# Attention steps reordered: the scores first, three kinds of transposes and small products behind them, the weighted sums last

## The chip, the cores and the metric

The kernel runs on one core of one Trainium2 chip. The metric is the time of one execution on the device, in microseconds (us). The engines are named as the profile names them: PE is TensorE's matrix multiplication, PEld its weight loads, DVE is VectorE, ACT is ScalarE, POOL is GpSimd, SP is SyncE, which here only issues DMAs.

## The reference

Three layers follow one another. Windowed attention has 4 batches, 8 heads, 576 positions and heads of 64; a position sees itself and the 63 before it. Its output, 2304 tokens of 512 columns, goes through a mixture of 8 experts, in which a token whose skip score is not positive keeps its value, and then through a block of two products.

```python
def _attn_ref(q, k, v):
    scores = scale * np.matmul(q, k.transpose(0, 1, 3, 2))
    mask = (rel >= 0) & (rel < window)
    scores = np.where(mask, scores, -1000000000.0)
    scores = scores - np.max(scores, axis=-1, keepdims=True)
    attn = np.exp(scores)
    attn = attn / (np.sum(attn, axis=-1, keepdims=True) + 1e-09)
    return np.matmul(attn, v).astype(np.float32)

def _moe_ref(x, w_skip, w_gate, w1, w2):
    do_compute = x @ w_skip > 0
    xc = x[do_compute]
    logits = xc @ w_gate
    e_idx = np.argmax(logits, axis=1)
    gate_w = probs[np.arange(len(xc)), e_idx]
    h = np.maximum(xc[mask] @ w1[e], 0.0)
    y[mask] = gate_w[mask, None] * (h @ w2[e])
    out[do_compute] = xc + y

def _moe2_ref(x, w_in, w_out):
    h = x @ w_in
    g = np.where(pos, h, np.where(neg, 0.0, (h + beta) ** 2 / (4.0 * beta)))
    return g @ w_out
```

## The kernel before

**Stages.** The attention takes the first 104 us, the experts the time to 340 us, the block the rest. All three stand in one program whose order on each engine is the order in which the code is written. The attention works in 18 steps `t` (NT = 18), one for each 128 tokens; a step's two groups of 64 tokens have the numbers 2t and 2t + 1 (`k` is 0 or 1). Work on one tile of tokens is spread over several steps, a few functions to each:

- `stage_s(t)`, the scores: masks by four bf16 products (L343), 32 products of 64 rows by 64 columns of q against the keys (L353), into two of three PSUM banks `s0` to `s2`; then on VectorE the row maxima (L360), one instruction for each group, and on ScalarE eight exponentials (L364) that take the maximum as bias.
- `stage_t(t)`: eight fp32 transposes of the probabilities (L378) into banks `pt0` and `pt1`. The copy of the first bank into SBUF (`pts`, group 2t, "even") is ScalarE's (L382), that of the second ("odd") VectorE's (L384). For tile 15 ScalarE makes both.
- `stage_v(t)`: 32 products of the transposed probabilities with the values `vt` (L406), 128 rows by 64 columns, into bank `o`; a column of ones in `vt` gives the row sums. VectorE normalises: `den` (L412), its reciprocal, a product into `x`. Then the loads of two further blocks of values go on SP's queue into the buffers just read (L313).
- `stage_x(t)`: four transposes of `x` (L429) into a score bank, copied to `xT` by VectorE (L437).
- `stage_l(t)`: four products of `xT` with the gate weights (L450), the logits, copied by VectorE (`ls`, L458). `stage_l2(t)`: one product that adds up their quarters (L464) into the bank `misc`.
- The ranks, for groups of 3, 3, 3, 4, 2 and 3 tiles (ROUTES): `route_a`, six VectorE operations from the logits to a one-hot choice (from L472), in steps 7, 10 and 13; a step later `route_b`, small products against a triangular matrix (L500 to L503) and four VectorE operations (L527 to L542) and `route_h`, GpSimd's selection tiles, and in the same step the gate, `route_g`, two VectorE operations from L575 on; three steps after `route_a` `route_c`, products (L604) and a sum. So `route_b` is in steps 8, 11 and 14 and `route_c` in 10, 13 and 16.

The fp32 transposes and the gate's products use the array in one tiling (128*128, the logits 128*32), the scores 64*64, the weighted sums 128*64: the profile prints that form in each row.

**The order of a step.** TensorE runs, in step t of the loop: weighted sums of tile t - 3, probability transposes of t - 2, rank products that are due, scores of t, the quarters' sum of t - 5, logits of t - 4, transposes of x of t - 3. VectorE and ScalarE have the matching order. Scaling of q for the next block (L328, ScalarE) stands ahead of the scores in the odd steps. At a step's end the loads of raw weights go on SP's queue, and in steps 3, 5, 6, 8, 9, 11, 12, 14 and 15 a finished load is split (L140 on ScalarE, the rest on GpSimd). The loop runs to step 16; step 17 and what remains of the pipeline are written out behind it.

```python
        for t in range(NT - 1):
            if t >= 3:
                stage_v(t - 3)
            if t >= 2:
                stage_t(t - 2)
            for f in due.pop(t, ()):
                f()
            if t % 2:
                scale_q(t // 2 + 1)
            stage_s(t)
```

Ahead of the loop 114 small products (WARM, L621) run while the first loads are under way.

## Time and profile before

| what | value |
| --- | --- |
| runs without a profile | 693.84, 694.4 and 698.65 us (median 694.4) |
| the profiled execution | 691.08 us, its span 689.3 us |
| PE busy | 661.5 us, 96% of the span |
| DVE busy | 427.6 us, 62% |
| ACT busy | 385.6 us, 56% |
| POOL busy | 93.2 us, 14% |
| mean granted TensorE clock | 0.999 |

The profile lists what each engine did in one execution. A busy share says how much of the span an engine worked, not what it waited for. The span runs from the first instruction to the last; the execution's time is 1.8 us longer. In the timeline a row is one stretch of like instructions: start, length, engine, line, operation, output and inputs by the program's names, form, count, and in brackets how long the engine stood idle ahead of it and what ended that. "issue" there means that nothing the profile shows was waited for. Lengths of matmuls that follow one another overlap, so the pace of TensorE is read from differences of starts.

### The profile page before, as it was taken

What the parts mean: (1) busy time and instruction counts of PE and PEld (TensorE: products, weight loads), DVE (VectorE), ACT (ScalarE), POOL (GpSimd) and SP (SyncE); (2) the same over time, 40 slices, a digit from 0 to 9 for tenths busy, and PEclk for the clock granted to TensorE, in tenths of its full rate; (3) what the DMA queues carried; (4) which work ended last, traced back from release to release, by engine and by line L of the source; (5) the groups of instructions that cost most, each with busy time, mean ns of one, the idle gap of its engine ahead of it and who ended that gap; (6) DMA issues with size and microseconds to landing.
All of it is one profiled execution on the core that took longest, in us unless ns stands there. A gap on an engine that the chain in (4) does not pass through costs nothing.

```text
span 689.3 us, 12283 instructions
## 1 busy us (share of the span) xinstructions
PE 661.5 (96%) x4633; PEld 567.9 (82%) x4633; DVE 427.6 (62%) x814; ACT 385.6 (56%) x769; POOL 93.2 (14%) x140
## 2 busy tenths in 40 slices
PE   7999989999989989989999999999999999999997
PEld 6787867777767766979899999999999999999995
DVE  5788876995963997877888844343434333433332
ACT  6787744763824773666666655454444454445442
POOL 3256546232312110000000000000000000000000
PEclk9999999999999999999999999999999999999999
DMA  8999838997872855323424003030300030002001
GB/s 258 291 276 295 256 116 287 325 341 252 283 294 69 281 216 191 112 87 108 123 92 138 1 1 76 16 78 16 92 1 0 1 93 0 1 1 47 0 1 46
DMA packets 34584, 88.93 MB, mean 129 GB/s; under 512 B 7014, under 2 KB 8166, under 8 KB 34500
## 3 DMA queue, kind: packets, MB, share of 16 engines
q1 hardware_dynamic: 26352, 74.34, 34.8%
q10 hardware_dynamic: 5748, 6.83, 3.1%
q0 software_dynamic: 2400, 6.68, 2.7%
q8 instruction: 48, 0.79, 0.5%
q14 instruction: 36, 0.29, 0.1%
HBM read 75.91 MB, written 13.12 MB: 129 GB/s over the span
## 4 chain that ended last, share of the span: by engine, by line
PE 52%; DVE 6%; ACT 2%; issue 1%; DMA 0%; ACTq 0%; DVEq 0%
PE po L1005 25%; PE h L977 25%; DVE c L998 2%; PE spare L1093 1%; ACT q L988 1%; DVE gs L996 1%; PE p2x L967 1%; DVE c L995 1%; DVE w L141 1%; DVE q L987 1%; DVE q L991 1%; DVE x2T L136 0%; DMA x<-x 0%; ACT q L984 0%; ACT gs L993 0%
## 5 line engine op out<-in xcount | busy, mean ns | idle before, releaser
L977 PE MATMUL h<-x2T,w 128*128 128x384 f32 x1152 | 218.0, 337 | 1.1 <-DVE x2T L136 1.1
L1005 PE MATMUL po<-w,gs 128*128 128x512 f32 x864 | 217.0, 395 | 1.7 <-ACT w L140 0.9
L977 PEld LDWEIGHTS h<-x2T,w 128*128 128x128 f32 x1152 | 204.5, 188 | 10.1 <-DVE x2T L136 1.7
L1005 PEld LDWEIGHTS po<-w,gs 128*128 128x128 f32 x864 | 159.5, 188 | 32.1 <-ACT w L140 1.2
L984 ACT ACTIVATE q<-h 128x384 f32<-128x384 f32 x96 | 46.9, 489 | 107.9 <-PE h L977 104.0
L987 DVE TENSOR_SCALAR q<-q 128x384 f32<-128x384 f32 x96 | 34.4, 358 | 97.9 <-ACT q L984 97.8
L991 DVE TENSOR_TENSOR q<-hs,q 128x384 f32<-128x384 f32 x96 | 53.7, 559 | 49.8 <-ACT q L988 49.8
L993 ACT ACTIVATE gs<-q 128x384 fp32r<-128x384 f32 x96 | 50.4, 525 | 60.0 <-DVE q L991 60.0
L996 DVE TENSOR_TENSOR gs<-q,gs 128x384 fp32r<-128x384 f32 x96 | 53.7, 559 | 44.3 <-ACT gs L993 44.3
L852 PE MATMUL y<-w,hT 128*128 128x512 f32 x264 | 70.2, 403 | 4.0 <-DVE hT L136 2.7
L140 ACT ACTIVATE w<-raw 128x1024 fp32r<-128x1024 f32 x64 | 65.4, 1058 | 15.4 <-PEq L924 4.7
L141 DVE TENSOR_TENSOR w<-raw,w 128x1024 fp32r<-128x1024 f32 x55 | 64.8, 1219 | 3.8 <-ACT w L140 1.9
L988 ACT ACTIVATE q<-q 128x384 f32<-128x384 f32 x96 | 50.5, 526 | 22.3 <-DVE q L987 18.8
L852 PEld LDWEIGHTS y<-w,hT 128*128 128x128 f32 x264 | 47.2, 188 | 17.2 <-DVE hT L136 4.4
L364 ACT ACTIVATE pr<-s,nb 128x128 f32<-128x128 f32 x144 | 39.0, 384 | 15.5 <-DVE nb L360 15.5
L986 ACT ACTIVATE hs<-h 128x384 f32<-128x384 f32 x96 | 46.8, 488 | 0.0
L813 PE MATMUL ha<-w,mxT 128*128 128x512 f32 x132 | 33.4, 399 | 3.5 <-DVE mxT L136 0.7
L813 PE MATMUL hb<-w,mxT 128*128 128x512 f32 x132 | 34.9, 400 | 0.0
L813 PEld LDWEIGHTS ha<-w,mxT 128*128 128x128 f32 x132 | 23.9, 188 | 12.2 <-issue 4.5
L777 POOL DMA_INDIRECT x<-mx,idx x11 | 16.5, 1497 | 105.4 <-POOLq L921 41.0
L360 DVE TENSOR_REDUCE nb<-s 128x4 f32<-128x512 f32 x36 | 23.2, 686 | 11.4 <-PE s L353 10.2
L813 PEld LDWEIGHTS hb<-w,mxT 128*128 128x128 f32 x132 | 24.0, 188 | 4.7
(182 smaller groups left out, 683.3 us busy)
## 6 DMA issues: line engine op xcount, KB each, us to landing
raw<-in_wu SPq DMA_DIRECT2D x62, 512.0 KB, 6.7
raw<-in_wd SPq DMA_DIRECT2D x31, 512.0 KB, 4.1
x<-x SPq DMA_DIRECT2D x21, 256.0 KB, 3.2
vt<-in_vs SPq DMA_DIRECT2D x36, 130.0 KB, 6.2
out<-out SPq DMA_DIRECT2D x36, 128.0 KB, 2.3
q<-in_qs SPq DMA_DIRECT2D x8, 512.0 KB, 5.2
kt<-in_ks SPq DMA_DIRECT2D x8, 512.0 KB, 6.8
x<-x ACTq DMA_DIRECT2D x16, 256.0 KB, 6.4
```

The costliest lines, as they stand in the source:

```text
L140: nc.scalar.activation(t[:, 0], src, AF.Copy)
L141: eng.tensor_tensor(t[:, 1], src, t[:, 0].bitcast(F32), ALU.subtract)
L813: nc.tensor.matmul(ph, lhsT=xT[:, a, c, :], rhs=halves[4 * e + j, c][:, b, :], start=(n == 0), stop=(n == len(seq) - 1),)
L852: nc.tensor.matmul(py, lhsT=hT[j][:, a, c, :], rhs=halves[4 * e + 2 + j, c][:, b, :], start=(j == 0 and n == 0), stop=(j == 1 and n == len ...
L977: nc.tensor.matmul(ph, lhsT=halves[U_IN + m // 4, c][:, b, (m % 4) * P : (m % 4 + 1) * P], rhs=xT[:, a, c, :], start=(n == 0), stop=(n == ...
L984: nc.scalar.activation(q, ph, AF.Relu, bias=0.5, scale=0.5)
L986: nc.scalar.activation(h, ph, AF.Copy)
L988: nc.scalar.activation(q, q, AF.Square)
L991: nc.vector.tensor_tensor(q, h, q, ALU.max)
L993: nc.scalar.activation(gs[:, 0], q, AF.Copy)
L996: dve.tensor_tensor(gs[:, 1], q, gs[:, 0].bitcast(F32), ALU.subtract)
L1005: nc.tensor.matmul(po[i], lhsT=gs[:, a, i * P : (i + 1) * P], rhs=w[:, b, :], start=(m == m0 and (a, b) == PASSES[0]), stop=(m == m1 - 1 a ...
```

## The change

The scores' stage is cut into three functions: `stage_s` keeps the products, `stage_m(t, k)` is one row maximum, `stage_e(t)` the exponentials. `stage_t` takes a function `between`, which it calls ahead of VectorE's copy: in the loop that is the first maximum, and the second follows the copy. TensorE's order of a step is now: scores of t, rank products that are due, probability transposes of t - 2, transposes of x of t - 3, quarters' sum of t - 5, logits of t - 4, weighted sums of t - 2. So the weighted sums of a tile stand in the same step as its transposes, where they stood in the next. `route_a` and the gate stand ahead of the sums. `xT` has two buffers. Behind the loop the scores, maxima and exponentials of step 17 stand ahead of the transposes of tile 15. The warm-up has 108 products. Lines behind the first edit move by 5 to 7: L360 is now L362, L364 L369, L378 L383, L382 L387, L384 L391, L406 L413, L412 L419, L429 L436, L437 L444, L450 L457, L458 L465, L464 L471.

```diff
@@ -55,7 +55,7 @@
 
 SLOW = (0, 1, 2, 4, 4, 6, 7, 8, 8)
 ROUTES = (3, 3, 3, 4, 2, 3)
-WARM = 114
+WARM = 108
 WARM_COLUMNS = 48
 PUT_OFF = 98
 WGW = 32
@@ -354,10 +354,15 @@
                             s[k][half * BLK : (half + 1) * BLK, p, :], lhsT=qt[i][r, b0 + k, p, :],
                             rhs=kt[r, e : o + 1 : o - e, b0 + k, p, :], start=False, stop=(p == 3),
                         )
-            nb = []
-            for k in range(2):
-                nb.append(sm.tile([P, 4], F32, tag="nb", name=f"nb{2 * t + k}"))
-                nc.vector.tensor_reduce(nb[k], s[k], axis=AX.X, op=ALU.max, negate=True)
+            st["s", t] = s, []
+
+        def stage_m(t, k):
+            s, nb = st["s", t]
+            nb.append(sm.tile([P, 4], F32, tag="nb", name=f"nb{2 * t + k}"))
+            nc.vector.tensor_reduce(nb[k], s[k], axis=AX.X, op=ALU.max, negate=True)
+
+        def stage_e(t):
+            s, nb = st.pop(("s", t))
             for k in range(2):
                 pr = ap2.tile([P, 4, P], F32, tag="pr", name=f"pr{2 * t + k}", bufs=4)
                 for p in range(4):
@@ -366,7 +371,7 @@
                     )
                 st["p", 2 * t + k] = pr
 
-        def stage_t(t):
+        def stage_t(t, between=None):
             last = t + 1 == NT
             if last:
                 both = ldp.tile([P, 2, 4, P], F32, tag="q", name="pts_last")
@@ -381,6 +386,8 @@
                 if last or k == 0 or t + 3 == NT:
                     nc.scalar.activation(pts, pt, AF.Copy)
                 else:
+                    if between:
+                        between()
                     nc.vector.tensor_copy(pts, pt)
                 st["pt", g] = pts
 
@@ -428,7 +435,7 @@
             for c in range(KD):
                 nc.tensor.transpose(px[:, c, :], x[:, c * P : (c + 1) * P], ident)
             if t + 3 < NT:
-                xT = ap2.tile([P, KD, P], F32, tag="xT", name=f"xT{t}", bufs=1)
+                xT = ap2.tile([P, KD, P], F32, tag="xT", name=f"xT{t}", bufs=2)
             elif t + 3 == NT:
                 xT = ap2.tile([P, KD, P], F32, tag="pr", name=f"xT{t}", bufs=4)
             else:
@@ -637,27 +644,31 @@
             of.update({f + i: (f, i, n, j % 2) for i in range(n)})
         due, since, gates = {}, {}, {}
         for t in range(NT - 1):
-            if t >= 3:
-                stage_v(t - 3)
-            if t >= 2:
-                stage_t(t - 2)
-            for f in due.pop(t, ()):
-                f()
             if t % 2:
                 scale_q(t // 2 + 1)
             stage_s(t)
+            for f in due.pop(t, ()):
+                f()
+            if t >= 2:
+                stage_t(t - 2, partial(stage_m, t, 0))
+                stage_m(t, 1)
+            else:
+                stage_m(t, 0)
+                stage_m(t, 1)
+            stage_e(t)
             if t == 3:
                 misc = psp.tile([P, 512], F32, tag="misc", name="misc")
             most[0] = 1 if t < 3 else 2 if t + 3 < NT else 3
             (load_q if t % 2 else load_k)(t // 2 + 2)
             if t >= 3:
                 store_t(t - 3, nc.scalar)
+
+            if t >= 3:
+                stage_x(t - 3)
             if t >= 5:
                 stage_l2(t - 5, *of[t - 5][1:])
             if t >= 4:
                 stage_l(t - 4)
-            if t >= 3:
-                stage_x(t - 3)
             if t >= 5:
                 tg, i, n, side = of[t - 5]
                 if i == n - 1:
@@ -671,6 +682,8 @@
                     gates[t + 1] = partial(route_g, tg, n)
             if t in gates:
                 gates.pop(t)()
+            if t >= 2:
+                stage_v(t - 2)
 
             if t:
                 load_raws()
@@ -680,9 +693,11 @@
             if t + 2 < NT and splits and since.get(splits[0][1:], t) + 2 <= t:
                 work(splits, [pool])
 
-        stage_v(NT - 4)
+        stage_s(NT - 1)
+        stage_m(NT - 1, 0)
+        stage_m(NT - 1, 1)
+        stage_e(NT - 1)
         stage_t(NT - 3)
-        stage_s(NT - 1)
         rows = kept(*ROWS_AT, RW)
         nc.gpsimd.memset(rows, 0.0)
         store_t(NT - 4, nc.sync)
```

**VectorE, step 8.** The rows run from the normalising of tile 5 (`x5`) to the copies of step 8; `nb16` and `nb17` are the row maxima of step 8, `pts13` the odd copy of tile 6, `r2`, `ps` and `rc` the ranks of `route_b`. Before:

```order
L412 TENSOR_SCALAR den5_923<-o5_922 128x8
L413 RECIPROCAL rec5_924<-den5_923 128x8
L414 TENSOR_TENSOR x5_925<-o5_922,rec5_924 128x512
L384 COPY pts13_959<-pt13_954 128x512
L527 TENSOR_TENSOR r2_0_968<-misc_515,oh0_914 128x27
L529 TENSOR_REDUCE ps0_970<-r2_0_968 128x3
L539 SCALAR_TENSOR_TENSOR rc0_972<-ps0_970,far_134 128x3
L542 SCALAR_TENSOR_TENSOR rc0_972<-rc0_972,ps0_970 128x3
L360 TENSOR_REDUCE nb16_1009<-s16_987 128x4
L360 TENSOR_REDUCE nb17_1011<-s17_988 128x4
L458 COPY ls4_1030<-misc_515 128x128
L437 COPY xT5_1037<-px5_1032 128x512
```

Now:

```order
L419 TENSOR_SCALAR den5_915<-o5_914 128x8
L420 RECIPROCAL rec5_916<-den5_915 128x8
L421 TENSOR_TENSOR x5_917<-o5_914,rec5_916 128x512
L534 TENSOR_TENSOR r2_0_970<-misc_509,oh0_908 128x27
L536 TENSOR_REDUCE ps0_972<-r2_0_970 128x3
L546 SCALAR_TENSOR_TENSOR rc0_974<-ps0_972,far_134 128x3
L549 SCALAR_TENSOR_TENSOR rc0_974<-rc0_974,ps0_972 128x3
L362 TENSOR_REDUCE nb16_1002<-s16_941 128x4
L391 COPY pts13_1001<-pt13_996 128x512
L362 TENSOR_REDUCE nb17_1005<-s17_942 128x4
L444 COPY xT5_1024<-px5_1019 128x512
L465 COPY ls4_1031<-misc_509 128x128
```

The copy `pts13` stood directly behind the normalising; now the four rank operations and a maximum stand ahead of it. `xT5` and `ls4` have changed places.

**TensorE, step 8.** `s16` and `s17` are the scores, `pt12` and `pt13` the transposed probabilities of tile 6, `px5` the transposes of x, `o5` and `o6` weighted sums. Before, the step began with the end of `o5` and the transposes, ahead of the rank products:

```order
L406 MATMUL o5_922<-vt3_164,pts11_852 64x65
L378 MATMUL pt12_947<-ident_71,pr12_784 128x128 x4
L378 MATMUL pt13_954<-ident_71,pr13_789 128x128 x4
L500 LDWEIGHTS stri_102
L500 MATMUL misc_515<-oh0_914,stri_102 128x27
```

and ended with these:

```order
L353 MATMUL s17_988<-kt_160,q4_699 64x128 x2
L464 MATMUL misc_515<-quarters_76,ls3_899 128x9
L450 MATMUL misc_515<-xT4_906,wg_sb_167 32x128 x4
L429 MATMUL px5_1032<-ident_71,x5_925 128x128 x4
L406 MATMUL o6_1047<-vt0_161,pts12_952 64x65
L406 MATMUL o6_1047<-vt1_162,pts13_959 64x65
```

Now its end, from the last rank product on, reads:

```order
L510 LDWEIGHTS ones_69
L510 MATMUL misc_509<-run_128,ones_69 128x27
L383 MATMUL pt12_989<-ident_71,pr12_778 128x128 x4
L383 MATMUL pt13_996<-ident_71,pr13_783 128x128 x4
L436 MATMUL px5_1019<-ident_71,x5_917 128x128 x4
L471 MATMUL misc_509<-quarters_76,ls3_900 128x9
L457 MATMUL misc_509<-xT4_893,wg_sb_167 32x128 x4
L413 MATMUL o6_1038<-vt0_161,pts12_994 64x65
L413 MATMUL o6_1038<-vt1_162,pts13_1001 64x65
```

The transposes have moved from ahead of the scores to the x transposes, and the sums of tile 6 follow in the same step, behind the logits.

**ScalarE, the end of the loop.** `pr34` and `pr35` are the exponentials of step 17, `pts30` and `pts31` the copies of tile 15, `ex0` an exponential of the gate in the part behind the loop. Before:

```order
L423 DMA x1_68<-kt_160 128x512
L382 ACTIVATE pts30_1934<-pt30_1929 128x512
L382 ACTIVATE pts31_1941<-pt31_1936 128x512
L364 ACTIVATE pr34_1969<-s34_1943,nb34_1965 128x128 x4
L364 ACTIVATE pr35_1974<-s35_1944,nb35_1967 128x128 x4
L490 ACTIVATE ex0_136<-d9_1997 128x4x8
```

Now:

```order
L430 DMA x1_68<-kt_160 128x512
L369 ACTIVATE pr34_1949<-s34_1923,nb34_1945 128x128 x4
L369 ACTIVATE pr35_1954<-s35_1924,nb35_1947 128x128 x4
L387 ACTIVATE pts30_1964<-pt30_1959 128x512
L387 ACTIVATE pts31_1971<-pt31_1966 128x512
L497 ACTIVATE ex0_136<-d9_1991 128x4x8
```

The two copies stood ahead of the eight exponentials and stand behind them.

## Rows read from the trace of the kernel before

**Rows 1.** Windows view: stretch, us, busy (instructions) by engine, PEclk, DMA share, GB/s.

```profile
21.00:85.00 64.00, 61.96 (x1199) 50.43 (x1203) 54.47 (x144) 50.03 (x139) 35.85 (x36) 1.00 0.98 281
```

**Rows 2.** Timeline, weight loads: start, us, what, xcount, [idle before <-releaser].

```profile
22.25 0.11 PEld L343 LDWEIGHTS <-ident_b 64*64 64x64 bf16 x4 [0.17 <-issue]
...
78.83 0.86 PEld L378 LDWEIGHTS pt<-ident,pr 128*128 128x128 f32 x8
79.65 0.41 PEld L604 LDWEIGHTS misc<-at,to 128*128 128x128 f32 x3
80.14 0.11 PEld L343 LDWEIGHTS <-ident_b 64*64 64x64 bf16 x4
...
81.36 0.30 PEld L464 LDWEIGHTS misc<-quarters,ls 128*128 128x128 f32 x2 [0.17 <-issue]
...
82.03 0.42 PEld L429 LDWEIGHTS px<-ident,kt 128*128 128x128 f32 x4 [0.20 <-issue]
82.62 1.01 PEld L406 LDWEIGHTS o<-vt,pts 128*64 128x64 f32 x32 [0.17 <-issue]
83.70 0.86 PEld L378 LDWEIGHTS pt<-ident,pr 128*128 128x128 f32 x8
84.72 0.11 PEld L343 LDWEIGHTS <-ident_b 64*64 64x64 bf16 x4 [0.17 <-issue]
```

**Rows 3.** Timeline, VectorE, step 8 and the end of step 7; one row later.

```profile
39.55 0.17 DVE L472 TENSOR_REDUCE m<-misc 128x3 f32<-128x24 f32 x1
...
40.70 0.16 DVE L412 TENSOR_SCALAR den<-o 128x8 f32<-128x8 f32 x1
...
41.74 0.68 DVE L384 COPY pts<-pt 128x512 f32<-128x512 f32 x1
42.34 0.17 DVE L527 TENSOR_TENSOR r<-misc,oh 128x27 f32<-128x27 f32 x1
...
43.11 1.29 DVE L360 TENSOR_REDUCE nb<-s 128x4 f32<-128x512 f32 x2
44.32 0.28 DVE L458 COPY ls<-misc 128x128 f32<-128x128 f32 x1
...
45.11 0.17 DVE L575 TENSOR_REDUCE sx<-ex 128x3 f32<-128x27 f32 x1
...
83.85 0.17 DVE L412 TENSOR_SCALAR den<-o 128x8 f32<-128x8 f32 x1 [0.22 <-PE o L406]
```

**Rows 4.** Timeline, ScalarE: a weight split; step 16 and the last exponentials.

```profile
45.99 1.06 ACT L140 ACTIVATE w<-raw 128x1024 fp32r<-128x1024 f32 x1
...
84.45 1.08 ACT L382 ACTIVATE pts<-pt 128x512 f32<-128x512 f32 x2
86.85 2.17 ACT L364 ACTIVATE pr<-s,nb 128x128 f32<-128x128 f32 x8 [1.31 <-DVE nb L360]
```

**Rows 5.** Timeline, TensorE and VectorE, from step 17 on.

```profile
87.20 1.41 PE L406 MATMUL o<-vt,pts 128*64 128x65 f32 x32
...
86.12 1.29 DVE L360 TENSOR_REDUCE nb<-s 128x4 f32<-128x512 f32 x2 [1.15 <-PE s L353]
...
89.39 0.16 DVE L412 TENSOR_SCALAR den<-o 128x8 f32<-128x8 f32 x1
```

**Rows 6.** Instructions of the tiles vt: how long their transfers take to land.

```profile
DMA to landing us min/median/max: 3.1/6.0/7.9
```

**Rows 7.** Timeline, TensorE: the warm-up and the first scores.

```profile
1.11 4.50 PE L621 MATMUL warm<-ones 128*128 128x48 bf16 x114 [1.11 <-DVE ones L203]
...
6.59 1.11 PE L353 MATMUL s<-kt,q 64*64 64x128 f32 x30 [0.64 <-ACT q L626]
```

**Rows 8.** Timeline, TensorE: matmuls of step 16.

```profile
82.03 0.66 PE L429 MATMUL px<-ident,kt 128*128 128x128 f32 x4
82.62 1.15 PE L406 MATMUL o<-vt,pts 128*64 128x65 f32 x32
83.70 1.09 PE L378 MATMUL pt<-ident,pr 128*128 128x128 f32 x8
```

## The prediction

> **What bounds the kernel now.** I began with the stretches: the diff touches only the attention, some 100 of 689 us, and there, from 21 to 85 us, TensorE is busy for 61.96 of 64 us [rows 1]. So a step costs what its products take, and I read them as TensorE's weight loads in order of time [rows 2]. The reader is to see the printed idle times ahead of a load: 0.17 us ahead of the rank scores L464, 0.20 ahead of the transposes of x L429, 0.17 ahead of the weighted sums L406, 0.17 ahead of the scores L343. Each stands where the array's tiling changes. From the first score load at 80.14 to the next at 84.72 a step without rank work takes 4.58 us: scores 1.22, rank scores and gate logits 0.67, transposes of x 0.59, weighted sums 1.08, transposes of the probabilities 1.02 (differences of starts). Next I read VectorE and ScalarE over the step whose rank work falls between its products [rows 3, 4], because both work in the order of the program: whatever is put ahead of a copy delays it. Then the end, where little runs beside the chain [rows 5], the value loads [rows 6] and the start [rows 7].
>
> **Removed: two changes of tiling a step.** New order: scores, probability transposes, x transposes, rank scores, logits, weighted sums. Four transposes are busy 0.66 us and eight 1.09 [rows 8], so one more costs 0.108. Twelve in a run, with a change at either end, take 0.59 + 8 x 0.108 = 1.45 us where the two stages took 0.59 + 1.02 = 1.61: 0.16 saved. The rank scores now follow in the same tiling; that junction isn't in the trace. Its saving lies between 0 and the 0.17 printed there; I take 0.09, half, because the first junction gave 0.16 and an ordinary load also needs some of the gap. A plain step comes to 4.33 us (bounds 4.21, if both idle times of 0.17 and 0.20 go whole, and 4.42).
>
> The Trainium skill says in "TensorEngine Tiling (Array Packing)", Tiling Modes, that changing the mode drains TensorE; "TensorE: Matmul & The Clock Gate", Part 2, puts a drain at about 128 cycles. At 2.4 GHz that is an estimate of 0.05 us a change, 1.4 us for two changes in 13 steps, where 0.25 a step from the rows makes 3.3. The rows show the idle time three times as long, so my sum goes by the rows.
>
> **Start.** Six warm-up products of 114 that take 4.50 us are 0.24 us. The first real score product waits until 6.59 for ScalarE's scaling of q with 0.64 us idle ahead of it [rows 7], so this is worth 0; uncovered it would gain 0.24. The granted clock is 1.00 (2.4 GHz) from 21 us on [rows 1]; no row shows it after a shorter warm-up, and the matmul of the first two steps at half that clock would cost at most some 3 us. The transposes of tile 0 go behind the scores of step 2; I take 0 for the first four steps, with 1 us either way, since the products that fill that wait now come after it.
>
> **Moved: what VectorE does in a step.** Pitches [rows 3]: a row maximum 0.605 (two from 43.11 to 44.32), rank-score copy and xT copy together 0.79, normalising a tile from `den` to the next copy 1.04, a pts copy 0.60, the six operations of `route_a` 1.15 (39.55 to 40.70), the four of `route_b` 0.77 (0.19 each, so about 0.4 for the gate's two). Plain step, scores beginning at 0: the maximum starts at 1.40 (86.12 against 84.72 [rows 2, 5]), the odd pts copy when its transposes end, about 2.40, and ends at 3.08; the weighted sums stand at 1.22 + 1.45 + 0.58 = 3.25 and don't wait. The second maximum ends its turn at 3.60, xT is done at 4.29, and the next scores, which reuse its bank, come at 4.33. It just fits.
>
> In a rank step (8, 11, 14) it does not. `route_a` was put ahead of the normalising in the step before, so `den` comes at 4.40 + 1.15 - 4.33 = 1.22 and VectorE is free at 2.26. Now `route_b` stands ahead of the maximum: 3.03. Maximum: 3.63. Only then the odd pts copy, done at 4.31. The weighted sums begin at 4.36, where TensorE alone (0.3 for `route_b`'s products) would be at 3.55; behind them xT is done at 5.51 and the next scores come at 5.55. Before, these copies had the whole of rank scores, logits and x transposes as cover; in the new order the copy has 0.85 us between transposes and sums. That cover gone costs 1.0 us in each of three steps.
>
> **Moved: ScalarE.** The even pts copy goes ahead of the exponentials and the bias of the first four comes from the first maximum. In a plain step that is hidden. In steps 9 and 15 a weight split (1.06 [rows 4]) and a scaling of q (as many elements, so as long) both stand ahead of that copy, behind exponentials that began late in the rank step. From 3.75, eight exponentials held by the second maximum until 6.03, the gate's store, split and scale: 8.5 to 8.6, that is 3.0 in the next step, copy done at 3.6, sums 0.4 late (bounds 0 and 0.8).
>
> Steps 10, 13 and 16 carry `route_c`: 1.31 between transposes (78.83) and scores (80.14) [rows 2] against 1.02, so 0.30. Steps 4 to 16 then: 4.02 (no rank scores yet, 0.31 less) + 3 x 4.33 + 3 x 5.55 + 2 x 4.73 + 3 x 4.63 + 4.33 = 61.34 us. Before they took 84.72 - 22.25 = 62.47 [rows 2]. **Gain 1.1 us.**
>
> **Moved: the end.** Before, the last loop products were the transposes of tile 15, whose two ScalarE copies were done (84.45 + 1.08) before the exponentials of step 17 began (86.85) [rows 4]. Now the exponentials come first. From step 17's scores: maximum at 1.40, eight exponentials from 2.13 taking 2.17, the next start about 4.20, two copies 1.08: 5.28, sums of tile 15 at 5.33 against 87.20 - 84.72 = 2.48 [rows 5]. Plain sums are busy 1.15 [rows 8] and `den` follows 0.08 later (83.85 behind the sums from 82.62 [rows 3, 8]): 6.56 against 89.39 - 84.72 = 4.67, where VectorE arrived late anyway because of `route_a`. **Loss 1.9 us**, all of it on the path: everything to the first expert hangs on this normalising and the ranks behind it. If VectorE's queue has something else there it could be 1.5; with all of the delay of the sums 2.8.
>
> **Nothing for:** the second buffer for xT (it allows logits behind x transposes), the new place of `stage_v` ahead of the weight loads on SP's queue (same number of loads per step), the maxima outside `stage_s`.
>
> **Sum.** -1.1 + 1.9 = +0.8 us. The profiled execution took 691.08 (span 689.3): 691.9. The median of the three runs shown is 694.4, 3.3 above it; on that scale 695.2. What comes after attention keeps its length: its matmuls don't wait for weights that the attention would have fetched, since the same splits stand in the same steps.
>
> **Rivals.**
> B, *TensorE's pace everywhere*: VectorE's and ScalarE's waits don't show, because in three steps VectorE's work is 3 x 3.64 (the pitches of a plain step added up) + 1.15 + 0.77 + 0.4 + 0.2 for the sum of `route_c` = 13.4 us, below TensorE's 3 x 4.33 + 0.6 = 13.6. Rank steps 4.63 and steps 9 and 15 4.33 take off 2.8 + 0.8: net -2.8, so 691.6. For it: VectorE has the room on average. Against it: the order above; an average doesn't move a copy forward. "TensorEngine Tiling (Array Packing)", Performance Considerations, of the Trainium skill warns that copies out of PSUM may become the bottleneck when products get faster; by these rows that is so in order, not in total.
>
> C, *slower: values land late*. The two loads go out when a tile's sums end and must have landed at the sums two steps on. At 4.88 a step that was 2 x 4.88 - 1.08 - 0.6 = 8.1 us after the second issue, at 4.33 it is 7.0. Landings take 3.1, 6.0, 7.9 us (least, median, most) [rows 6]. It decides when the typical landing passes 7.0; at 7.9 each pair of steps is 0.9 late, 5.9 over 13 steps, less what the rank steps cover (1.2): +4.7 to the sum, 699.9. For it: the DMA engines are 0.98 busy from 21 to 85 us [rows 1]. Against it: the median has 1 us in hand, and a step's raw weights now queue behind the values, not before.
>
> D, *the change doesn't do what it says*: the idle time is not that of the tiling but of the stage before it ending, and comes back at the new junctions. Steps of 4.58, then 13 x 0.25 = 3.3 more: 698.5. Against it: where products of `route_c` (L604) follow the transposes L378 with no change of tiling, at 79.65, no idle time is printed [rows 2].
>
> **How the numbers follow.** My sum 0.55 (its own range, from the bounds of junction, start and end: 693 to 698), B 0.25, C 0.10, D 0.10. The predicted time is the likeliest's, 695.2. The range 690 to 699.5 holds it, B and D and about half of C, some 0.87 in all with the spread of the runs. One per cent is 6.9 us, about what a measurement of this kernel can tell from no change (its runs lie 693.84 to 698.65). Faster than that would need more than twice B: 0.03. Slower needs C beyond its price: 0.07. Within: 0.90.
>
> **What would show it.** Right: plain steps near 4.33 between first score loads, two printed idle times fewer a step; steps 8, 11 and 14 near 5.5 with TensorE waiting ahead of L413 for VectorE's pts L391; step 17's scores about 1 us earlier than 84.72; the sums of tile 15 waiting for ScalarE's pts L387 until about 5.3 us after those scores. Wrong: rank steps under 5.0 (B); L413 released by DMA of vt (C); idle time ahead of L436 or L471 as large as before (D); an end of attention more than 2 us from the old one.

## The result and the profile after

The changed kernel took 699.44 us in the median of 20 executions (696.43 to 702.15), the kernel before 695.24 in as many. One execution of the kernel before took 734.67 us and stands apart from its other 19 (691.31 to 698.65). The ratio is 1.006, with a 95% interval of 1.0044 to 1.0077: some 4.2 us slower (3.1 to 5.4). The forecast was +0.8 us, a change of less than 1%. The sign was right and the change stayed under 1%; the size fell short by some 3.4 us, and these are the subject of what follows. The median lies only just inside the range of 690 to 699.5.

The page of the changed kernel: its span, busy times and the row of granted clocks, 40 slices of 17.5 us.

```profile
span 700.4 us, 12279 instructions
...
PE 665.2 (95%) x4627; PEld 573.5 (82%) x4627; DVE 428.7 (61%) x814; ACT 387.1 (55%) x769; POOL 93.7 (13%) x140
...
PEclk8899999999999999999999999999999999999999
```

TensorE's busy time is longer by 3.7 us (661.5 before) although it does six products less, and the row of clocks, which was all nines before, begins with two eights. The profiled execution is at the slow end of its kind (702.15), as that of before (691.08) was at the fast end of its own; so the two spans, 11.1 us apart, show more than the 4.2 us that the change costs. Where the 11.1 lie:

| between | before | changed | difference |
| --- | --- | --- | --- |
| start and scores of step 4 | 22.25 | 25.84 | +3.6 |
| scores of step 4 and of step 17 | 62.47 | 63.99 | +1.5 |
| scores of step 17 and weighted sums of tile 17 | 10.34 | 12.25 | +1.9 |
| those sums and the first product of the experts | 13.24 | 13.90 | +0.7 |
| that product and the end of the span | 581.0 | 584.4 | +3.4 |

Up to the first product of the experts (L813, now L828) the end of the attention has so lost 2.6 us. The 0.7 of the fourth line goes to a copy of logits behind the sums:

```profile
108.15 0.45 ACT L463 ACTIVATE ls<-pl 128x128 f32<-128x128 f32 x2 [0.82 <-PE lg_end L471]
```

The kernel before makes its copies there without that wait. The fourth line is 13.2 in all four profiles of the old order, 13.9 to 14.3 in five of the new and 13.2 in the other five; what decides between them is not shown.

How much of the last line is the change's is not shown. Over 13 profiles of kernels that are alike behind the attention (all of this study but a_fill, below) that stretch took 581.0 to 584.4 us. Some 1.6 us of the difference belong to a lower granted clock from 310 to 320 us, 0.83 in this profile and 1.00 in that of before: the products of the block (L977, now L992) span 408.8 us with it and 407.2 without. The stretch is inside the block, whose first product comes at 270 us in the kernel before, not at 340. Seven of the 13 profiles have it, two of them in the old order (b_start and b_fill); whether the new order makes it more frequent can't be told. Without it the stretch is 581.0 to 581.6 us in the four profiles of the old order and 581.7 to 582.9 in the nine of the new: some 0.6 us that no run explains.

**The start.** The timeline of TensorE in the changed kernel (start, us, line, operation, tiles, form, count, idle time before and its releaser):

```profile
10.49 0.40 PE L343 MATMUL s<-mask_first,ident_b 64*64 64x512 bf16 x2 [2.57 <-ACT pr L369]
...
13.56 0.63 PE L343 MATMUL s<-mask_odd,ident_b 64*64 64x512 bf16 x2 [1.63 <-ACT pr L369]
13.56 2.33 PE L353 MATMUL s<-kt,q 64*64 64x128 f32 x32
15.83 1.97 PE L383 MATMUL pt<-ident,pr 128*128 128x128 f32 x8
...
25.84 0.41 PE L343 MATMUL s<-mask_even,ident_b 64*64 64x512 bf16 x4
```

and its windows (stretch, us, busy of PE, PEld, DVE, ACT, POOL with instructions, PEclk, DMA share, GB/s):

```profile
5.00:12.00 7.00, 3.72 (x90) 2.87 (x87) 3.16 (x6) 3.56 (x12) 1.46 (x4) 1.00 0.98 258
12.00:23.00 11.00, 9.02 (x112) 7.68 (x113) 4.00 (x9) 6.26 (x19) 0.00 (x0) 0.53 0.74 230
```

TensorE waits twice for ScalarE's exponentials, 2.57 us up to 10.49 and 1.63 us up to 13.56, with little between. Behind that the granted clock is 0.53 from 12 to 23 us, which is 1.2 GHz but for the ends. The 32 products of the scores are busy 2.33 us there and 1.11 in the first step [rows 7]; the eight transposes 1.97 us against 1.09 [rows 8]. In the kernel before the transposes of tile 0 stood in the second gap and the clock was 1.00 in its profile:

```profile
12.00:23.00 11.00, 9.31 (x186) 7.44 (x188) 7.81 (x16) 10.06 (x30) 0.47 (x1) 1.00 1.00 303
```

**A plain step.** Weight loads of step 5 of the changed kernel, to be laid beside [rows 2]:

```profile
31.34 0.86 PEld L383 LDWEIGHTS pt<-ident,pr 128*128 128x128 f32 x8 [0.17 <-issue]
32.16 0.47 PEld L436 LDWEIGHTS px<-ident,x 128*128 128x128 f32 x4
32.60 0.30 PEld L471 LDWEIGHTS misc<-quarters,ls 128*128 128x128 f32 x2
32.92 0.16 PEld L457 LDWEIGHTS misc<-xT,wg_sb 128*32 128x32 f32 x8
33.28 1.02 PEld L413 LDWEIGHTS o<-vt,pts 128*64 128x64 f32 x32 [0.20 <-issue]
34.37 0.16 PEld L343 LDWEIGHTS <-ident_b 64*64 64x64 bf16 x4
```

Two idle times are printed, ahead of the probability transposes (0.17) and ahead of the weighted sums (0.20), where there were four; none is left ahead of the x transposes and of the quarters' product. From scores to scores the engine's rows give 4.28 us (30.13 to 34.41) in steps 4, 5, 7 and 12. The next scores come right behind VectorE's copy of xT, which frees their bank; it ends at 34.36:

```profile
33.68 0.68 DVE L444 COPY xT<-px 128x512 f32<-128x512 f32 x1
```

**A rank step.** VectorE in step 8, to be laid beside [rows 3], and the weight loads that wait for it:

```profile
47.35 0.17 DVE L534 TENSOR_TENSOR r<-misc,oh 128x27 f32<-128x27 f32 x1
...
48.12 0.68 DVE L362 TENSOR_REDUCE nb<-s 128x4 f32<-128x512 f32 x1
48.72 0.68 DVE L391 COPY pts<-pt 128x512 f32<-128x512 f32 x1
49.32 0.68 DVE L362 TENSOR_REDUCE nb<-s 128x4 f32<-128x512 f32 x1
...
48.62 0.19 PEld L413 LDWEIGHTS o<-vt,pts 128*64 128x64 f32 x2 [0.20 <-issue]
49.46 1.01 PEld L413 LDWEIGHTS o<-vt,pts 128*64 128x64 f32 x30 [0.65 <-DVE pts L391]
```

The order is the one forecast: normalising, `route_b`, a maximum, and only then the odd copy, which ends at 49.40. The sums, two of which had begun with the even group, go on at 49.46 and name that copy. Steps 8, 11 and 14 took 5.55, 5.49 and 5.48 us. In these three 0.16 us of idle time is also left ahead of the x transposes (L436).

**Step 9.** ScalarE, and the sums that wait for it:

```profile
51.90 0.41 ACTq L585 DMA_DIRECT2D x<-gate  x1
52.36 1.06 ACT L140 ACTIVATE w<-raw 128x1024 fp32r<-128x1024 f32 x1 [1.12 <-DVE x L421]
53.33 1.04 ACT L328 ACTIVATE q<-q 128x1024 f32<-128x1024 f32 x1
54.27 0.58 ACT L387 ACTIVATE pts<-pt 128x512 f32<-128x512 f32 x1
...
54.90 1.08 PEld L413 LDWEIGHTS o<-vt,pts 128*64 128x64 f32 x32 [1.30 <-ACT pts L387]
```

The weight split (L140) starts 1.12 us after ScalarE had become free, the scaling of q and the even copy stand behind it, and the sums wait 1.30 us. The step takes 5.41. The profile names VectorE's x for the 1.12 us, which the split doesn't read. What stands right ahead of the split in ScalarE's order is the issue of the gate's store (L585), and the split follows its end, 52.31, by 0.05 us. It does so in the other profiles too (52.21 and 52.25 in a_tail, 52.65 and 52.69 in a_rankb). The gate itself was ready at 51.10; what holds the issue until 51.90 is not shown.

**Step 6** took 6.40, and no engine is to blame. The timeline of TensorE:

```profile
37.57 1.03 PE L413 MATMUL o<-vt,pts 128*64 128x65 f32 x27
40.50 0.39 PE L413 MATMUL o<-vt,pts 128*64 128x65 f32 x5 [1.90 <-issue]
```

For 1.90 us it waits for nothing that the profile shows, between two products of one kind. The kernel before has such a stop too, 0.97 us up to 21.89 in its first profile and 1.04 us, also in the sums of tile 4, in its second (b_again, below).

**The end.** ScalarE, weight loads and VectorE from step 17 on, to be laid beside [rows 4, 5]:

```profile
92.00 2.18 ACT L369 ACTIVATE pr<-s,nb 128x128 f32<-128x128 f32 x8 [1.58 <-DVE nb L362]
94.01 1.14 ACT L387 ACTIVATE pts<-pt 128x512 f32<-128x512 f32 x2
...
94.71 0.19 PEld L413 LDWEIGHTS o<-vt,pts 128*64 128x64 f32 x2 [1.75 <-ACT pts L387]
95.20 1.01 PEld L413 LDWEIGHTS o<-vt,pts 128*64 128x64 f32 x30 [0.30 <-ACT pts L387]
...
96.39 0.17 DVE L419 TENSOR_SCALAR den<-o 128x8 f32<-128x8 f32 x1 [1.19 <-PE o L413]
```

The exponentials come first, the two copies of tile 15 after them, and the weighted sums begin with the first copy and go on with the second, 5.37 us after the scores of step 17 (89.83). `den` comes at 6.56.

### The profile page after: what moved, and what is told of

Same layout as the page of the kernel before. It is cut to its first block, busy times and chain, and to the rows that moved or that the text cites. A ratio compares the mean times of both kernels' runs of the same rounds, so it can differ in the third digit from the quotient of the medians.

```text
span 700.4 us, 12279 instructions
## 1 busy us (share of the span) xinstructions
PE 665.2 (95%) x4627; PEld 573.5 (82%) x4627; DVE 428.7 (61%) x814; ACT 387.1 (55%) x769; POOL 93.7 (13%) x140
## 4 chain that ended last, share of the span: by engine, by line
PE 51%; DVE 6%; ACT 2%; DMA 1%; issue 1%; SPq 0%; ACTq 0%; DVEq 0%
PE po L1020 25%; PE h L992 25%; DVE c L1013 2%; ACT q L1003 1%; DVE gs L1011 1%; DVE c L1010 1%; PE p2x L982 1%; DVE w L141 1%; DMA x<-x 1%; DVE q L1002 1%; DMA x<-mx,idx 1%; DVE q L1006 1%; DVE x2T L136 0%; ACT q L999 0%; ACT gs L1008 0%
## 5 line engine op out<-in xcount | busy, mean ns | idle before, releaser
L992 PE MATMUL h<-x2T,w 128*128 128x384 f32 x1152 | 218.0, 337 | 1.1 <-DVE x2T L136 1.1
L992 PEld LDWEIGHTS h<-x2T,w 128*128 128x128 f32 x1152 | 204.7, 188 | 10.1 <-DVE x2T L136 1.7
L140 ACT ACTIVATE w<-raw 128x1024 fp32r<-128x1024 f32 x64 | 65.3, 1056 | 17.1 <-PEq L939 4.7
L369 ACT ACTIVATE pr<-s,nb 128x128 f32<-128x128 f32 x144 | 40.4, 380 | 6.3 <-DVE nb L362 5.2
L828 PE MATMUL ha<-w,mxT 128*128 128x512 f32 x132 | 33.4, 399 | 4.0 <-issue 0.8
L828 PE MATMUL hb<-w,mxT 128*128 128x512 f32 x132 | 35.0, 400 | 0.0
L828 PEld LDWEIGHTS ha<-w,mxT 128*128 128x128 f32 x132 | 23.9, 188 | 12.7 <-issue 5.7
L413 PE MATMUL o<-vt,pts 128*64 128x65 f32 x544 | 23.0, 230 | 8.2 <-ACT pts L387 4.3
L413 PEld LDWEIGHTS o<-vt,pts 128*64 128x64 f32 x544 | 19.7, 142 | 12.8 <-ACT pts L387 5.7
```

The source lines that it names most:

```text
L140: nc.scalar.activation(t[:, 0], src, AF.Copy)
L828: nc.tensor.matmul(ph, lhsT=xT[:, a, c, :], rhs=halves[4 * e + j, c][:, b, :], start=(n == 0), stop=(n == len(seq) - 1),)
L992: nc.tensor.matmul(ph, lhsT=halves[U_IN + m // 4, c][:, b, (m % 4) * P : (m % 4 + 1) * P], rhs=xT[:, a, c, :], start=(n == 0), stop=(n == ...
```

## The experiments

All are the kernel before or the changed kernel with an edit or two. In all, ratios are to the kernel before, timed beside it on the same chip; its median was 694.83, 696.57, 696.04 and 695.26 us in the four series. The mean clock is that of TensorE over one whole execution, so a lower clock at 310 to 320 us counts in it as one at the start does. The table gives its median over the executions: 92 of the kernel before (range 0.989 to 1.000), 20 of the changed one (0.987 to 0.994). Over those 92 executions of one kernel the time falls by 0.48 us for each 0.001 of mean clock (least squares, correlation -0.52). By this the step from 0.9945 to 0.990 is an estimate of 2.2 us.

| kernel | edit | ratio | 95% interval | mean clock |
| --- | --- | --- | --- | --- |
| before | | 1 | | 0.9945 |
| changed | | 1.006 | 1.0044 to 1.0077 | 0.990 |
| a_start | changed, tile 0's transposes ahead of the scores | 1.0018 | 0.9992 to 1.0043 | 0.993 |
| b_start | before, tile 0's transposes behind the scores | 1.0092 | 1.0058 to 1.0125 | 0.988 |
| a_fill2 | changed, gaps at the start filled | 1.001 | 0.9982 to 1.0038 | 0.997 |
| b_fill | before, gap at the start filled | 1.0021 | 0.9991 to 1.005 | 0.995 |
| a_warm | changed, warm-up of 114 | 1.007 | 1.0038 to 1.0102 | 0.990 |
| a_tail | changed, copies ahead of exponentials at the end | 1.0031 | 1.0003 to 1.006 | 0.990 |
| a_rank | changed, rank work behind the maxima | 1.0091 | 1.0066 to 1.0117 | 0.990 |
| a_ranklate | changed, all rank work at a step's end | 1.0118 | 1.0081 to 1.0154 | 0.987 |
| a_rankb | changed, `route_b` alone at a step's end | 1.0077 | 1.0052 to 1.0103 | 0.989 |
| a_all | a_start, a_ranklate and a_tail together | 1.0057 | 1.0031 to 1.0083 | 0.990 |
| a_fill | changed, gaps filled with 84 more products | 1.024 | 1.0207 to 1.0273 | 0.983 |

### The start: does the idle time bring the lower clock, and what does it cost?

**a_start** puts one stage back to its old place, in one step:

```diff
+            if t == 2:
+                stage_t(0)
             stage_s(t)
             for f in due.pop(t, ()):
                 f()
-            if t >= 2:
+            if t > 2:
                 stage_t(t - 2, partial(stage_m, t, 0))
```

> The changed kernel with one thing undone: in step 2 the transposes of tile 0 stand ahead of the scores again (there they fill TensorE's wait for the exponentials). In the changed kernel's profile TensorE stood idle for 1.63 us up to 13.56 and the granted clock was 0.50 from 12.5 to 22.5 us. Theory 'start': the idle time brings the lower clock in most executions; then the clock stays 1.00 here, the scores of step 4 begin 3 to 4.5 us earlier than 25.84, and the ratio to the kernel before is 0.999 to 1.002 instead of 1.006. Rival 'chance': the clock at the start falls in some executions of any of these kernels; then the ratio stays at 1.005 to 1.007.

**b_start** does the opposite to the kernel before: `stage_t(0)` behind `stage_s(2)`.

> The kernel before with only the transposes of tile 0 moved behind the scores of step 2. Theory 'start': an idle stretch of 1 us or more up to about 13.5 us, the granted clock at 0.50 behind it for some 10 us, the scores of step 4 some 3 to 4 us later than 22.25, ratio 1.004 to 1.006. Rival 'chance': clock 1.00 as often as not, ratio 0.999 to 1.002.

Ratios 1.0018 and 1.0092: the place of these eight transposes alone is worth 2.9 us in the changed kernel and costs 6.4 us in the old one, more than the 1.004 to 1.006 expected. In the profiles the scores of step 4 began at 23.62 in a_start, 2.2 ahead of the changed kernel (3 to 4.5 expected), and at 28.80 in b_start, 6.55 after those of the kernel before (3 to 4 expected; a stop of 1.95 us is among them). The windows of a_start:

```profile
5.00:12.00 7.00, 2.66 (x58) 1.95 (x59) 2.77 (x5) 2.40 (x9) 1.43 (x4) 0.81 0.95 256
12.00:23.00 11.00, 10.39 (x178) 8.63 (x175) 6.25 (x12) 9.10 (x27) 0.00 (x0) 0.81 0.86 248
```

and of b_start:

```profile
5.00:12.00 7.00, 3.29 (x93) 2.75 (x90) 2.77 (x5) 3.42 (x12) 1.43 (x4) 1.00 0.98 254
12.00:23.00 11.00, 7.66 (x90) 6.45 (x83) 3.80 (x8) 5.73 (x19) 0.00 (x0) 0.50 0.71 215
```

In b_start the clock is down for the whole stretch, as in the changed kernel. In a_start it did not stay at 1.00, as I had expected: in this execution it was down too, 0.81 in either window; it fell within a gap of TensorE of 3.88 us that ended at 11.78. This profile, 701.34 us, is the slowest of its twelve executions (median 696.73), with a mean clock of 0.987. So the times bear out theory 'start', and this one profile bears out that the clock also falls in executions in which these transposes stand in their old place. A second profile of the kernel before says the same.

**b_again**, the kernel before without an edit:

> The kernel before, unchanged, for a second profile. If the lower clock at the start comes by chance in any kernel, it may show here between 8 and 25 us; if it comes from the idle time that the new order leaves, the clock is 1.00 there and the scores of step 4 begin at 22.25 +- 0.5 us.

```profile
12.00:23.00 11.00, 11.00 (x188) 9.02 (x184) 7.60 (x15) 8.64 (x28) 0.00 (x0) 0.81 0.87 272
```

0.81 again, in both windows (1.2 GHz between 9 and 17 us), and the scores of step 4 began at 22.68, 0.43 later than in the first profile and within the half microsecond named. The first profile has its stop of 0.97 us ahead of these scores and the second has none there, so the clock cost it some 1.4 us. So 'chance' is right in part. What differs is how often and how late: 19 of 20 executions of the changed kernel have a mean clock of 0.992 or less, and 17 of 92 of the kernel before.

**a_fill2** leaves the new order as it is and gives TensorE something to do in the two gaps:

```diff
-WARM = 108
+WARM = 94
...
+        wide = ones.rearrange("p (o k) -> p o k", o=1).to_broadcast([P, 4, P])
...
+            for _ in range((0, 8, 6)[t] if t < 3 else 0):
+                nc.tensor.matmul(warm_up[:, 0:4], lhsT=ones, rhs=wide, start=True, stop=True)
             stage_s(t)
```

> The changed kernel with the idle time of TensorE at the start filled: 8 wide products of no use (512 columns) ahead of the scores of step 1 and 6 ahead of those of step 2, and 14 products fewer in the warm-up, so that the program has as many instructions as the changed kernel (a_fill, which had 84 more, stood still for 4.1, 2.9, 3.9 and 2.4 us in the experts where the changed kernel doesn't). Theory 'idle time brings the lower clock': mean granted clock of the executions 0.993 to 0.997 instead of 0.990, the scores of step 4 at 21.5 to 23 us in the profile, ratio 1.001 to 1.003. Rival: the lower clock comes from something else in the new order (the steps with waits, the end); mean clock 0.990, ratio 1.006.

```profile
5.00:12.00 7.00, 5.14 (x83) 3.08 (x80) 3.30 (x6) 3.99 (x12) 1.43 (x4) 1.00 0.99 262
12.00:23.00 11.00, 9.85 (x177) 7.54 (x179) 7.29 (x15) 9.28 (x29) 0.00 (x0) 1.00 0.90 264
```

The clock is 1.00 in both windows, the mean clock 0.997, the scores of step 4 begin at 22.03 instead of 25.84, and the ratio falls from 1.006 to 1.001. Nothing in the order is changed, and 14 idle products are added: so it is the idle time, by way of the clock, that costs the changed kernel about 3.5 us by the two ratios, whose intervals leave 1 to 6. This is the cost against a clock that stays up, and not against the kernel before, which has part of the same loss: its median mean clock is 0.9945, that of a_fill2 0.997.

A profile of another run shows the new order at the full clock with nothing filled in. a_ranklate (below) has the changed kernel's order at the start. In the one execution profiled it has both waits, the first of them shorter, and the clock stayed at 1.00 (TensorE's timeline, then a window):

```profile
9.78 0.40 PE L343 MATMUL s<-mask_first,ident_b 64*64 64x512 bf16 x2 [1.88 <-ACT pr L369]
...
12.84 0.40 PE L343 MATMUL s<-mask_odd,ident_b 64*64 64x512 bf16 x2 [1.63 <-ACT pr L369]
...
12.00:23.00 11.00, 9.46 (x193) 7.89 (x193) 7.04 (x15) 9.34 (x28) 0.00 (x0) 1.00 0.99 293
```

Its scores of step 4 began at 21.48, 4.4 us ahead of those of the changed kernel and no later than in the kernel before. So the order and its waits as such cost next to nothing at the start; what costs is the lower clock, in the executions in which it comes.

The Trainium skill says in "TensorE: Matmul & The Clock Gate", Part 1, that the clock follows how busy TensorE has been of late, and that one kernel meets it differently from execution to execution. The two profiles of the kernel before, at 1.00 and at 0.81 from 12 to 23 us, agree.

**a_fill** was the first try of the same, with 84 products of the warm-up's small kind and the warm-up as it was.

> The changed kernel with idle work added and nothing moved: 48 products of the warm-up's kind ahead of the scores of step 1 and 36 ahead of those of step 2, where TensorE waited 2.6 and 1.6 us. Theory 'idle time at the start brings the lower clock': the granted clock stays 1.00 up to 30 us, the scores of step 4 begin near 22 instead of 25.84 us, ratio 1.000 to 1.002. Rival 'the order itself': the clock or no clock, the scores of steps 3 and 4 come late because the transposes of tile 0 stand behind those of step 2; then step 4 begins above 24.5 and the ratio is 1.004 or more.

By the ratios, 1.024 and 1.006, it is 12.5 us slower than the changed kernel. In its profile the scores of step 4 began at 24.70, above the rival's 24.5; but a wait of 1.99 us had stayed ahead of the scores of step 2 and the clock was 0.84 from 12 to 23 us, so it doesn't tell the two apart. The waits of TensorE (line, releaser: us, times, longest):

```profile
PE ha L830 <- PEq L938: 14.0, 5, 4.1
```

14.0 us go to waits of the experts for TensorE's own sequencer at L938 (a branch), where the longest of the changed kernel is 0.4 us. The same computation follows; only the number of instructions ahead of it has changed. Hence the exchange, product for product, in a_fill2.

**b_fill** fills the one long gap of the kernel before: 8 wide products ahead of `stage_s(1)`, 8 fewer in the warm-up.

> The kernel before with 8 wide products of no use ahead of the scores of step 1, where TensorE waited 2.4 us, and 8 fewer in the warm-up, so that the count of instructions stays. Its own executions had mean granted clocks of 0.989 to 1.000, median 0.9945, and a second profile showed the clock at 0.50 from 9 to 16.5 us. Theory 'idle time at the start brings the lower clock, in either kernel': mean clock 0.997 or more, ratio 0.996 to 0.999; against the changed kernel filled in the same way (a_fill2, ratio 1.001) it is 1.5 to 3 us faster, which is what the new order costs at an equal clock. Rival 'the kernel before loses nothing at the start, because it waits for transfers there': ratio 0.999 to 1.001 whatever the clock does.

The theory's numbers did not come: ratio 1.0021, with an interval that takes in 1, and a mean clock of 0.995 instead of 0.997. The ratio is also a little above the rival's 0.999 to 1.001. Since the clock was not held, the run doesn't settle between them. In the profile the clock was 1.00 up to 30 us, the scores of step 4 began at 21.75, and behind a stop of 1.93 us like that of step 6 the clock was 0.50 to 0.56 from 30 to 33 us. Filled alike, the two orders can't be told apart: 1.001 and 1.0021. The comparison at an equal clock that I had wanted, 1.5 to 3 us, is smaller than these intervals.

**a_warm** undoes the shorter warm-up.

> The changed kernel with the warm-up's 114 products back instead of 108. The prediction took this edit as worth nothing: ratio 1.005 to 1.007, mean granted clock 0.990. If the shorter warm-up had part in the lower clock, the clock comes back to 0.992 or more and the ratio to 1.004 or less.

Ratio 1.007, mean clock 0.990: the six products have no part in it.

### The end

**a_tail** gives ScalarE the two copies before the exponentials:

```diff
         stage_m(NT - 1, 1)
-        stage_e(NT - 1)
         stage_t(NT - 3)
+        stage_e(NT - 1)
```

> The changed kernel with the transposes and copies of tile 15 ahead of the exponentials of step 17 on ScalarE (scores and maxima stay ahead). By the prediction's sum the weighted sums of tile 15, which began 4.88 us after the scores of step 17 and waited for ScalarE's copies, begin 2.9 to 3.1 us after them, and the normalising follows at 4.7 instead of 6.1: 1.4 to 1.9 us less up to the first expert. Rival: the exponentials, now later, hold the sums of tiles 16 and 17 back as long; then those begin within 0.3 us of 9.95 and 12.25 us after the scores, and nothing is gained.

Its ScalarE, weight loads and VectorE from step 17 on (its scores at 89.75):

```profile
91.72 1.08 ACT L387 ACTIVATE pts<-pt 128x512 f32<-128x512 f32 x2 [1.39 <-PE pt L383]
92.69 2.17 ACT L369 ACTIVATE pr<-s,nb 128x128 f32<-128x128 f32 x8
...
93.05 1.01 PEld L413 LDWEIGHTS o<-vt,pts 128*64 128x64 f32 x32 [0.17 <-ACT pr L369]
...
95.03 0.16 DVE L419 TENSOR_SCALAR den<-o 128x8 f32<-128x8 f32 x1
```

Sums at 3.30 after the scores (expected 2.9 to 3.1), `den` at 5.28 (expected 4.7), where the changed kernel has 4.88 and 6.56. The sums of tile 17 begin 10.96 after the scores and not 12.25: 1.3 us. `den` now stands directly behind `route_a` on VectorE, which holds it 0.6 longer than I had counted. The first product of the experts comes 24.2 us after the scores of step 17, where the kernel before has 23.6 and the changed kernel 26.2. By the ratios, 1.0031 against 1.006, it is 2 us, with intervals of 2 us either way. Of the 1.9 us lost up to the sums of tile 17 ScalarE's order has 1.3, and the rival falls. The 0.7 behind them is gone here too, but so it is in profiles that leave the end alone (a_rank, a_ranklate).

### The rank steps

**a_rank** moves what is due behind the maxima:

```diff
             stage_s(t)
-            for f in due.pop(t, ()):
-                f()
             if t >= 2:
                 stage_t(t - 2, partial(stage_m, t, 0))
                 stage_m(t, 1)
...
+            for f in due.pop(t, ()):
+                f()
             stage_e(t)
```

> The changed kernel with the rank work of a step (products, VectorE's four operations, the selection tiles) behind both row maxima instead of ahead of the probability transposes. By the prediction's sum steps 8, 11 and 14, measured at 5.55, 5.48 and 5.49 us between first score loads, come to 4.6 to 4.8 and step 9 (5.40) to 4.4 to 4.7: 2.6 to 3.3 us less, ratio 1.001 to 1.003. Rival: VectorE's total work bounds those steps wherever the rank work stands; then they stay above 5.2 and the ratio at 1.006.

Missed: steps 8, 11 and 14 took 6.35, 5.54 and 5.54 us, and 10, 13 and 16 rose from 4.64 to 5.66. A new wait took the old one's place, here in step 8 (weight loads):

```profile
47.17 0.30 PEld L471 LDWEIGHTS misc<-quarters,ls 128*128 128x128 f32 x2 [1.40 <-DVE r L534]
```

The quarters' product writes the same bank, `misc`, from which VectorE's `route_b` (`r`, L534) still has to read.

**a_ranklate** moves all that is due to the end of a step, behind `stage_v`.

> The changed kernel with the rank work of a step moved to its end, behind the weighted sums and their normalising, so that it stands ahead of no copy that the step's sums wait for, nor ahead of the quarters' product, which waited 0.9 to 1.2 us for VectorE's rank operations where that work stood behind the maxima (a_rank). Theory: the rank steps are bound by VectorE's order; steps 8, 11 and 14 come from 5.5 to 4.6 to 4.9 us, 1.8 to 2.7 us less in all, ratio 1.002 to 1.0035. Rival: VectorE's total bounds them; then the lost time comes back in the step behind (8 and 9 together stay above 10.5 us) and the ratio at 1.006.

The ratio is 1.0118. Its profile, 697.20 us, is the fastest of its six executions (median 704.16), with a mean clock of 0.996 where the median is 0.987; even so steps 4 to 16 took 66.26 us in it, 2.3 more than in the changed kernel. Step 11 fell to 4.66 as expected, but step 8 only to 5.16, and steps 10, 13 and 14 rose to 6.14, 7.56 and 6.28. In 10 and 13 the gather lists' products (L611) now wait for the one-hot work of the same step:

```profile
71.65 0.41 PEld L611 LDWEIGHTS misc<-at,to 128*128 128x128 f32 x3 [2.90 <-POOL w L141]
...
69.36 1.77 DVE L483 SCALAR_TENSOR_TENSOR first<-d,desc 128x24 f32<-128x24 f32 x1
...
71.38 0.16 DVE L489 SCALAR_TENSOR_TENSOR pick<-misc,pick 128x3 f32<-128x3 f32 x1
...
66.41 4.67 POOL L141 TENSOR_TENSOR w<-raw,w 128x1024 fp32r<-128x1024 f32 x2
```

The load at 71.65 follows the last read of `misc` by VectorE (L489 at 71.38). VectorE itself was held up: L483, 0.18 us in the changed kernel, lasted 1.77 us and ended at 71.13, right behind GpSimd's two splits (66.41 + 4.67). The Trainium skill says in "SBUF — State Buffer", section "SBUF: two separate sides", that GpSimd and a VectorE operation with two inputs in SBUF shut each other out of a port for a whole instruction; L483 is such a one, and the trace agrees.

**a_rankb** leaves the gather lists where they were and moves only `route_b` and the selection tiles.

> The changed kernel with only the rank products, VectorE's four operations on them and the selection tiles at a step's end; the products of the gather lists stay behind the scores (in a_ranklate they too stood at the end and waited 1.4 to 2.8 us there for VectorE). Theory: VectorE's order binds steps 8, 11 and 14; they come from 5.5 to 4.6 to 4.9 us, steps 10, 13 and 16 stay at 4.65, 1.8 to 2.7 us less in all. Rival: VectorE's total binds them; then 8 and 9, 11 and 12, 14 and 15 together take as long as before (10.9, 9.8 and 10.1 us). The mean granted clock of the executions should be that of the changed kernel, 0.990, in either case, so the ratio comes to 1.002 to 1.0035 or stays at 1.006.

Steps 11 and 12 took 9.80 us together (9.77 in the changed kernel), 14 and 15 10.08 (10.09), 8 and 9 11.29 (10.96). The time leaves the rank step and comes back in the next: the rival's numbers. Steps 11 and 12 are the clean pair. In 9 the sums wait 1.7 us for ScalarE's copy, at the start of 14 L483 is held up by GpSimd again (0.97 us), and 13 and 16 rose to 4.93 and 5.13. The windows of the changed kernel over steps 11 to 13 and over two plain steps test the rival's reason:

```profile
60.70:75.10 14.40, 13.84 (x279) 12.06 (x278) 13.02 (x38) 11.94 (x34) 9.64 (x11) 1.00 1.02 299
25.84:34.41 8.57, 8.52 (x178) 7.39 (x179) 7.43 (x16) 7.45 (x22) 2.37 (x1) 1.00 0.78 204
```

VectorE is busy 13.02 of 14.40 us in those three steps; in two plain ones it is 7.43 of 8.57. The same three steps took 14.66 in the kernel before, with VectorE busy 13.01. But TensorE is busy 13.84 of the 14.40, more than VectorE. Three steps at the plain pace of 4.28 with 0.3 and 0.36 us of rank products would come to 13.5, and VectorE's 13.02 would fit into that. So VectorE's total by itself doesn't make them 14.40, and the rival's reason is not shown. What the runs show is that some 0.9 us a group of three steps is lost, that none of the three other places for the rank work gave it back, and that each made new waits.

### Together

**a_all** joins a_start, a_ranklate and a_tail.

> The changed kernel with three places mended together: the transposes of tile 0 ahead of the scores of step 2 (a_start), the rank work at a step's end (a_ranklate), the copies of tile 15 ahead of the exponentials of step 17 (a_tail). Theory: the three causes add up, about 3 + 2.2 + 1.3 to 2 us off the changed kernel: ratio to the kernel before 0.996 to 0.998. Rival: they hide one another behind the transfers; ratio 1.000 or more.

It missed the expectation, 1.0057, because a_ranklate is a loss. Against a_ranklate alone (1.0118) it is 0.6% faster, 4.2 us, where a_start and a_tail gave 0.42% and 0.29%: within the intervals these two add up. In its profile steps 4 to 16 took 71.47 us, with the granted clock down to between 0.76 and 0.92 from 50 to 90 us. The two without the rank edit were not run; by the sums they would stand about level with the kernel before. No version here beat it.

## Why the prediction was right, and where it was short

- **Plain step.** Forecast 4.33, measured 4.28: the rank scores' junction lost its gap whole, where I had taken half. The size is right; the reason is not TensorE's products alone. Step 4, which has no rank scores yet, took 4.28 too, where 4.02 was forecast. By the rows VectorE's copy of xT sets the pace, which the prediction had at 4.29 as "It just fits".
- **Rank steps.** Forecast 5.55, 5.55, 5.55, measured 5.55, 5.49, 5.48, with the wait at the copy that was named. Steps 10, 13 and 16 came to 4.64 (4.63). The numbers and the wait were right. I called it the order, and moving the rank work did move the waits; but no place that was tried took them away, and why not is open.
- **Steps 9 and 15.** Forecast 4.73 each, measured 5.41 and 4.60. ScalarE's queue it was, with the gate's store, the split and the scaling that the prediction lists; in step 9 the store's issue came late and the split with it. The step took less in a_tail (4.89) and a_fill2 (4.95).
- **The loop.** Forecast 61.34 us for steps 4 to 16. Measured 63.99, or 62.1 without the stop of 1.90 in step 6; 61.6 and 61.8 in a_tail and a_warm without theirs. The kernel before has 62.5, and 62.25 in its second profile without its stop. So the gain was 0.2 to 0.9, not 1.1.
- **The end.** Forecast 1.9 at `den`, 6.56 against 4.67; measured 6.56 exactly. a_tail shows the cause of most of it. Up to the first product of the experts it is 2.6, within the bounds of 1.5 and 2.8; that `den` came out to the hundredth is luck, since the sums began at 4.88 and went on at 5.37 where one start at 5.33 was forecast.
- **The start.** This step failed: "I take 0 for the first four steps, with 1 us either way". I looked for what fills the wait and not for what the empty wait does to the clock. The text had the price at hand (the matmul of two steps at half the clock, some 3 us) but tied it to the shorter warm-up, which a_warm shows to be worth nothing. By a_fill2 the lower clock costs the changed kernel about 3.5 us. The kernel before has part of it, so the term of the sum is less: 2.2 us by the estimate from the mean clocks, not all of which need lie at the start.

With these the sum reads -0.2 to -0.9 for the loop, +2.6 for the end and +2.2 for the clock: 3.9 to 4.6, and 0.6 more with the stretch behind, against 4.2 measured (3.1 to 5.4). That the range held is in part luck. The sum's own range, 693 to 698, did not hold 699.44; the whole range reached to 699.5 for the sake of rivals C and D, and neither happened: no sums wait for the values, and in plain steps the gaps at the old junctions are gone. Rival B fell by the rank steps. Two of the signs named spoke against the sum: in the profile the scores of step 17 came 5.1 us later and not 1 earlier, and the sums of tile 17 came 7.0 us later, beyond the 2 us that were to show it wrong. Of both, 3.6 us lie ahead of step 4.

What stays open: the stops of TensorE of 0.8 to 2.0 us, between 20 and 43 us, that no releaser explains. Twelve of the 14 profiles have one, the kernel before included; whether the new order makes them longer can't be told from one profile of each.

## What to carry to other kernels

A product that is moved out of a wait leaves TensorE idle there, and what that costs is not only the wait: look whether the granted clock of the next 10 us holds, in more than one execution, and keep cheap work in the gaps of the start. When removed gaps make TensorE faster, add up the next engine's work over the stretch before placing things in it: where VectorE was busy 13.0 of 14.4 us and TensorE 13.8, moving VectorE's work only moved the waits from one step to the next. A mean clock over a whole execution doesn't say where the clock fell; read it by windows. At the end of a loop a queue of copies and exponentials is on the path in its written order; put first what the next products wait for.

## What the runs showed of the hardware that I had not expected

- The granted clock fell to 1.2 GHz behind gaps of TensorE of 2.57 and 1.63 us with 1.5 us of products between them, and stayed there for some 10 us though TensorE was busy 9.02 of the 11 us from 12 to 23. Behind gaps of 1.88 and 1.63 us in the same places (a_ranklate) it stayed at 1.00.
- Two executions of one unchanged kernel differ in it: 1.00 and 0.81 in the window from 12 to 23 us, scores of step 4 at 22.25 and 22.68.
- With 84 more small products at the start of the program (and as many weight loads) TensorE waited 14.0 us in five waits for its sequencer at a branch, 100 us later and beyond; with the number of instructions unchanged the longest was 0.4.
- In seven of 13 profiles the granted clock was also down, to between 0.83 and 0.88, from 310 to 320 us, far behind anything that was changed; it cost some 1.6 us.
- One VectorE operation of 0.18 us lasted 1.77, 0.97 and, in a_all, 1.21 and 1.77 us beside GpSimd's splits.
